# A first batch's near scores as one 64x64 product per head, and a new written-out order of the first 34 steps

## The chip, the core and the metric

The kernel runs on one core of a Trainium2 chip. The metric is the device time of one execution in microseconds. The core has a matrix engine (TensorE, PE in the profile; PEld is its loading of stationary operands), a vector engine (VectorE, DVE), an activation engine (ScalarE, ACT), a general engine (GpSimd, POOL), and a queue engine (SyncE, SP) whose instructions here only start DMA transfers. Each engine executes its own list of instructions strictly in the order in which it was written; semaphores make it wait for other engines. What stands behind a waiting instruction waits too.

## The reference

The computation is attention of two kinds over q, k, v of 8 batches, 8 heads, 576 positions, 64 elements a head, added up, followed by a two-layer network on all 4608 tokens.

```python
def _attn_ref(q, k, v):
    ...
    q_d = q.reshape(B, H, Sd, factor, D).mean(axis=3)      # and k_d, v_d; factor is 4
    out_d = sm_attn(q_d, k_d, v_d)                          # softmax attention on 144 means
    out_up = np.repeat(out_d, factor, axis=2)
    mask = np.abs(pos[:, None] - pos[None, :]) < factor     # near: 7 keys a query
    scores = scale * np.matmul(q, k.transpose(0, 1, 3, 2))
    scores = np.where(mask, scores, -1000000000.0)
    ... # softmax
    out_local = np.matmul(attn, v)
    return (out_up + out_local).astype(np.float32)

def _moe_ref(x, w_in, w_out, alpha):                        # x: 4608 x 512
    h = x @ w_in                                            # 512 x 2048
    g = np.maximum(h, 0.0) + alpha * np.minimum(h, 0.0)
    return (g @ w_out).astype(np.float32)
```

The two weight matrices arrive as 8-byte floats.

## The kernel before

**Steps of the network.** The tokens are cut into 18 chunks of 256, and the 2048 hidden columns into 8 pairs of 128-wide blocks, which gives 144 steps s = 0 to 143: chunk s // 8, pair s % 8. A step is `hidden` (24 matmuls of 128x256 into one of two PSUM banks, L971), `below` (ACT, L977) and `leak` (DVE, L993), which together apply the sloped activation, `split` (ACT, L999) and `spill` (POOL, L1005), which cut the result into a high and a low part, and `product` (12 matmuls of 128x512, L1033). High and low parts take the place of full float32 products: three matmuls for each. Since there are two banks for `hidden`, the `hidden` of step s + 2 can begin only when the `leak` of step s has read its bank.

**Weights.** Each pair's block of w_in (named `i0` to `i7`) and w_out (`o0` to `o7`) is loaded as raw 8-byte words (two DMAs, tile `raw`, three slots in turn) and turned into high and low parts by four operations: `convert` (ACT, L316), `bits` (DVE, L326), `upper` (ACT, L330) and `lower` (DVE, L336). `convert` writes a scratch tile, `temp`, of which there is one; the next `convert` waits until `bits` has read it. A slot of `raw` is free for the next load when `bits` has read it.

**First batch.** Tokens of batch 0 go first, since step 0 needs them. Their attention is done in four pairs of heads, `p0` to `p3`, with operations named `p0.turn00` and so on: `load0` and `load1` (q and k, tile `fqk`), `load2` (v, tile `fv`), `load3` (v in windows of 70 rows, tile `vw`), `turn` (PE transposes, tile `f0T` for q and `f1T` for k) and `turned` (ACT copies them to `qb` and `kT`), `near` (the masked near scores on PE, 9 windows of 64 queries and 70 keys, in two groups of 7 and 2, tile `fs`), `shift`, `near_exps` and `weights` (softmax, DVE and ACT), `over` and `kept` (turning the weights, tiles `fpt` and `fpT`), `near_weigh` (product with v, tile `fpv`), and beside them the 144-wide attention (`fold`, `flip`, `operands`, `scores`, `peak`, `exps`, `invert`, `scaled`, `across`, `held`, `weigh`, `store`). `join`, `high` and `low` put both together into `xx`, the operand of `hidden`. In `near` (L546 to L556), both heads of a pair lie on the 128 partitions, 64 each. The queries are put into `qb` block-diagonally: a window is 128 columns, of which the first 64 hold head 0 on partitions 0 to 63 and zeros below, the last 64 zeros and head 1 on partitions 64 to 127. One product of 128 by 128 with the 70 keys gives both heads' scores.

**Later batches** use other code: the near part on DVE (units `u3`, `u4`, ..., operations `multiply`, `total`, `first`, `weigh`, `gather`, `last`, lines L805 to L869) and the 144-wide part in pieces named `d10` (batch 1, pair 0), `d11` and so on, with their own loads (tile `ld`).

**Order.** Every operation has a due time in steps. The functions are called in the order of these times, which fixes the order on every engine and on SP's queue. For the first 34 steps (`HORIZON`) the due times come from the table `ORDER`, a list of 1027 names; behind it they come from rules, which the change does not touch.

Of the kernel before, what the change touches and what calls it, by code (L numbers as in the profile page):

```python
# [55 lines left out]
d10.load.0 o0.upper p0.invert p0.fold_v p1.near0 p0.scaled d10.load.1 o0.lower p0.kept0 p0.kept1 d10.load.3 p1.load3
p0.across0 p1.shift0 i1.convert p0.across1 p0.over2 o1.load p1.shift1 p0.held1 p0.near_weigh0 p0.kept2 i1.bits
p1.near_exps0 p3.load0 p1.near_exps1 p0.held0 p2.turn00 p1.weights i1.upper p0.weigh p2.turned00 p3.load1 d10.fold.0
p1.flip p0.store d10.fold.1 p2.turn10 p1.operands p0.near_weigh1 p2.turned10 o2.load i1.lower p2.turn04 d10.load.4
p2.turn14 d10.load.2 p2.turned04 p2.fold0 p1.scores p2.load2 p2.turned14 p2.fold1 p3.load2 p2.near0 o1.convert  # L60
p1.peak p1.fold_v p1.exps i2.load o1.bits p1.invert p0.join0 i3.load o1.upper p3.turn00 p2.shift0 p1.scaled
p0.near_weigh2 o1.lower p2.flip p2.near_exps0 p1.across1 p0.high0 p0.join2 p2.operands p0.low0 p1.across0 p1.held1
p0.join1 d10.fold.4 p2.near1 p1.held0 p0.high1 p0.low1 p1.over0 p3.turned00 p2.shift1 d10.fold.2 p2.near_exps1
p1.over1 p1.kept0 p2.weights d10.fold.3 p1.over2 p1.kept1 p3.turn04 p1.kept2 p3.turn10 p3.fold0 p3.turned04
# [1168 lines left out]
```

## Time and profile before

| | us |
|---|---|
| runs | 940.55, 941.21, 2989.08 |
| median | 941.21 |
| profiled execution: its time | 941.03 |
| profiled execution: span from first to last instruction | 939.2 |
| PE busy | 905.7 (96%) |
| DVE busy | 775.4 (83%) |
| POOL busy | 539.5 (57%) |
| ACT busy | 425.1 (45%) |
| chain that ended last, by engine | PE 73%, DVE 15%, ACT 4% |

The execution lasted 1.8 us longer than the span that its profile covers. The span has two parts: the first 86 us, in which batch 0's attention is made and the first weights are decoded, and the steps behind, in which PE hardly rests. A group of instructions shows its busy time, then the mean duration of one in ns, then the idle time ahead of it and who ended that. A row of the timeline that ends in square brackets tells how long the engine stood idle ahead of the instruction, and for whom.

### The profile page before, as it was taken

What the parts mean: (1) busy time and instruction counts of PE and PEld (TensorE: products, weight loads), DVE (VectorE), ACT (ScalarE), POOL (GpSimd) and SP (SyncE); (2) the same over time, 40 slices, a digit from 0 to 9 for tenths busy, and PEclk for the clock granted to TensorE, in tenths of its full rate; (3) what the DMA queues carried; (4) which work ended last, traced back from release to release, by engine and by line L of the source; (5) the groups of instructions that cost most, each with busy time, mean ns of one, the idle gap of its engine ahead of it and who ended that gap; (6) DMA issues with size and microseconds to landing.
All of it is one profiled execution on the core that took longest, in us unless ns stands there. A gap on an engine that the chain in (4) does not pass through costs nothing.

```text
span 939.2 us, 17607 instructions
## 1 busy us (share of the span) xinstructions
PE 905.7 (96%) x6402; PEld 833.4 (89%) x6402; DVE 775.4 (83%) x1389; ACT 425.1 (45%) x1069; POOL 539.5 (57%) x683
## 2 busy tenths in 40 slices
PE   5788999999999999999999999999999999999998
PEld 5676889898998999999999999999999999999997
DVE  5667679999997799998999889899998899997111
ACT  5588764524453453444443434444444442323221
POOL 2033476748757658667667476677657654525221
PEclk9998999999999999999999999999999999999999
DMA  7976733433343322522432433332424322210000
GB/s 176 209 237 199 261 95 87 132 111 100 105 129 101 90 83 69 157 83 83 129 98 73 133 91 105 105 105 71 139 85 117 107 72 66 78 35 24 1 24 22
DMA packets 63194, 98.25 MB, mean 105 GB/s; under 512 B 23556, under 2 KB 28932, under 8 KB 63108
## 3 DMA queue, kind: packets, MB, share of 16 engines
q1 hardware_dynamic: 62916, 96.88, 34.8%
q8 instruction: 50, 0.82, 0.4%
q10 hardware_dynamic: 192, 0.26, 0.1%
q14 instruction: 36, 0.29, 0.1%
HBM read 87.67 MB, written 9.44 MB: 103 GB/s over the span
## 4 chain that ended last, share of the span: by engine, by line
PE 73%; DVE 15%; ACT 4%; SPq 2%; DMA 2%; POOL 2%; issue 1%; ACTq 0%; DVEq 0%; POOLq 0%
PE h L971 33%; PE o L1033 32%; DVE qk L805 3%; DVE ls L809 3%; DVE t L993 2%; PE s L390 2%; DVE lb L866 2%; DVE pv L863 2%; PE pv L424 2%; ACT temp L316 1%; PE xp L875 1%; PE pT L414 1%; DMA raw<-in_moe_w_in 1%; DMA raw<-in_moe_w_out 1%; DVE xf L887 1%
## 5 line engine op out<-in xcount | busy, mean ns | idle before, releaser
L971 PE MATMUL h<-xx,wih 128*128 128x256 f32 x2304 | 332.7, 278 | 3.8 <-DVE t L993 3.0
L1005 POOL TENSOR_TENSOR gl<-t,gh 128x512 fp32r<-128x512 f32 x142 | 182.5, 1285 | 263.8 <-ACT gh L999 248.4
L971 PEld LDWEIGHTS h<-xx,wih 128*128 128x128 f32 x2304 | 297.9, 192 | 10.8 <-ACT woh L330 2.5
L993 DVE SCALAR_TENSOR_TENSOR t<-t,rise,h 128x256 f32<-128x256 f32 x288 | 124.8, 475 | 86.2 <-ACT t L977 85.7
L1033 PE MATMUL o<-woh,gh 128*128 128x512 f32 x576 | 184.0, 390 | 0.4 <-ACT sg L1040 0.4
L1033 PE MATMUL o<-woh,gl 128*128 128x512 f32 x576 | 177.6, 379 | 1.1 <-POOL gl L1005 1.1
L1033 PE MATMUL o<-wol,gh 128*128 128x512 f32 x576 | 177.5, 379 | 0.0
L971 PE MATMUL h<-xx,wil 128*128 128x256 f32 x1152 | 176.1, 276 | 0.0
L999 ACT CAST gh<-t 128x512 fp32r<-128x512 f32 x144 | 89.4, 621 | 181.1 <-PE o L1033 88.1
L977 ACT ACTIVATE t<-h 128x512 f32<-128x512 f32 x144 | 85.9, 596 | 160.4 <-PE h L971 130.1
L368 POOL TENSOR_TENSOR ld<-ld 72x256 f32<-72x256 f32 x167 | 124.4, 745 | 48.9 <-DMA ld<-in_q 29.6
L971 PEld LDWEIGHTS h<-xx,wil 128*128 128x128 f32 x1152 | 152.2, 192 | 0.0
L809 DVE TENSOR_REDUCE ls<-qk 128x12 f32<-128x768 f32 (+1 forms) x126 | 135.7, 1082 | 2.4
L1033 PEld LDWEIGHTS o<-woh,gl 128*128 128x128 f32 x576 | 108.8, 189 | 16.9 <-POOL gl L1005 1.5
L1033 PEld LDWEIGHTS o<-wol,gh 128*128 128x128 f32 x576 | 108.9, 189 | 14.9
L1033 PEld LDWEIGHTS o<-woh,gh 128*128 128x128 f32 x576 | 99.8, 190 | 11.2 <-issue 2.2
L866 DVE TENSOR_TENSOR lb<-lb,pv 128x384 f32<-128x384 f32 x168 | 94.8, 564 | 4.6
L805 DVE TENSOR_TENSOR qk<-k,qp 128x768 f32<-128x768 f32 (+1 forms) x78 | 83.5, 1076 | 0.3 <-ACT qp L799 0.2
L863 DVE TENSOR_TENSOR pv<-v,lb 128x1152 f32<-128x1152 f32 x84 | 79.5, 952 | 2.4
L189 POOL TENSOR_TENSOR xx<-xf,xx 128x256 fp32r<-128x256 f32 (+3 forms) x47 | 43.7, 934 | 25.2 <-ACT xx L901 25.2
L805 DVE TENSOR_TENSOR qk<-k,lb 128x768 f32<-128x768 f32 (+1 forms) x48 | 51.6, 1078 | 0.0
L887 DVE TENSOR_TENSOR xf<-xp,od 128x128 f32<-128x128 f32 (+3 forms) x110 | 39.9, 414 | 5.5 <-POOL xx L189 3.0
(148 smaller groups left out, 1009.8 us busy)
## 6 DMA issues: line engine op xcount, KB each, us to landing
...
raw<-in_moe_w_in SPq DMA_DIRECT2D x16, 512.0 KB
raw<-in_moe_w_out SPq DMA_DIRECT2D x16, 512.0 KB
ld<-in_q SPq DMA_DIRECT2D x56, 144.0 KB
ld<-in_k SPq DMA_DIRECT2D x56, 144.0 KB
ld<-in_v SPq DMA_DIRECT2D x56, 144.0 KB
```

The costliest lines, as they stand in the source:

```text
L368: e.tensor_tensor(lv[:, :, 0:128], lv[:, :, 0:128], lv[:, :, 128:256], op=ALU.add)
L805: nc.vector.tensor_tensor(st["qk", half, d0][:, :nd], window(tiles[u, "k"], half, d0, nd), st["qp", half].unsqueeze(1).to_broadcast([128, ...
L809: nc.vector.tensor_reduce(out=st["s"][:, half, d0:d0 + nd, :].rearrange("p a b -> p (a b)"), in_=st.pop(("qk", half, d0))[:, :nd].rearrang ...
L863: nc.vector.tensor_tensor(st["pv", half, d0][:, :nd], window4(tiles[u, "v"], half, d0, nd), prob(half, d0, nd), op=ALU.mult)
L866: nc.vector.tensor_tensor(st["acc"], st["acc"], st["pv", half, d0][:, i], op=ALU.add)
L887: nc.vector.tensor_tensor(xf.rearrange("p a t (s e) -> p e t a s", e=2)[:, par, k0:k0 + nk], tp.rearrange("p (t s e a) -> p e t a s", t=4, ...
L971: nc.tensor.matmul(ph[:, j], w[:, m, 128 * o:128 * o + 128], x[:, part, m], start=(i == 0), stop=(i == 11))
L977: nc.scalar.activation(t, hs[st], AF.Relu, scale=-1.0)
L993: nc.vector.scalar_tensor_tensor(t[:, j], t[:, j], rise[:, f:f + 1], h[:, j], op0=ALU.mult, op1=ALU.add)
L999: nc.scalar.copy(gh, t)
L1005: (nc.vector if f"s{st}.split" in ON_VECTOR else nc.gpsimd).tensor_tensor(gl, t, f32(gh), op=ALU.subtract)
L1033: nc.tensor.matmul(outs[c][m], g[:, j, 128 * m:128 * m + 128], wo[w][n][:, :, o].rearrange("p e a -> p a e"), start=(f == 0 and i == 0), s ...
```

## The change

The near scores of the first batch are written as two products of 64 by 64 a window, one for each head, in place of one of 128 by 128. `qb` loses its zero blocks (half its size, no memsets on DVE), and each `turned` of q is one ACT operation on 128 partitions in place of two on 64. The table `ORDER` has the same 1027 names in another order. In the diff, the table is cut to its first line.

```diff
 ORDER = """
-clear p0.load0 masks p0.load1 i0.load p1.load0 p0.turn00 p0.load3 p0.turn04 p0.turned00 p0.fold0 p0.turned04
...
+p0.load0 masks p0.load1 clear p0.load2 p1.load0 p1.load1 p0.turn00 p0.turn04 p0.turned00 i0.load p0.fold0
...
 """.split()
...
-        qb = st.tile([128, NWIN, 2, WIN], F32, name="qb")
-        nc.vector.memset(qb[0:64, :, 1, :], 0.0)
-        nc.vector.memset(qb[64:128, :, 0, :], 0.0)
+        qb = st.tile([128, NWIN, WIN], F32, name="qb")
...
             def turned(x, t0):
                 ps = s.pop(("turn", x, t0))
                 if x == 0:
-                    for e, r in enumerate(halves):
-                        nc.scalar.mul(
-                            qb[r, :, e, :].rearrange("p w (a t) -> p w a t", t=8)[:, :, :, t0:t0 + 4],
-                            ps[r].rearrange("p (t w a) -> p w a t", t=4, w=NWIN), SCALE)
+                    nc.scalar.mul(qb.rearrange("p w (a t) -> p w a t", t=8)[:, :, :, t0:t0 + 4],
+                                  ps.rearrange("p (t w a) -> p w a t", t=4, w=NWIN), SCALE)
...
                 for j in range(nw):
                     w = w0 + j
-                    nc.tensor.matmul(ps[:, KEYS * j:KEYS * j + KEYS], qb[:, w].rearrange("p e i -> p (e i)"),
-                                     kT[:, WIN * w:WIN * w + KEYS], start=False, stop=(j == nw - 1))
+                    for r in halves:
+                        nc.tensor.matmul(ps[r, KEYS * j:KEYS * j + KEYS], qb[r, w], kT[r, WIN * w:WIN * w + KEYS],
+                                         start=False, stop=(j == nw - 1))
```

The order shifts on every engine. Three places follow. The first is SP's queue around the load of the weight block i1 (`raw0_1`; `raw1` is a block of w_out). `fqk2` is q and k of pair 2, `fqk3` those of pair 3, `fv` and `vw` are v, `ld1_0` loads for batch 1. Before:

```order
L496 DMA fqk1_159<-in_k 72x8x64 x2
L274 DMA raw1_0_210<-in_moe_w_out 128x2048 x2
L514 DMA vw2_214<-in_v 70x9x64 x2
L501 DMA fv0_230<-in_v 72x2x512
L501 DMA fv1_237<-in_v 72x2x512
L514 DMA vw3_249<-in_v 70x9x64 x2
L270 DMA raw0_1_261<-in_moe_w_in 128x2x1024 x2
L496 DMA fqk2_281<-in_q 72x8x64 x2
L496 DMA fqk2_281<-in_k 72x8x64 x2
L358 DMA ld1_0_0_324<-in_q 72x512
L358 DMA ld1_0_1_343<-in_q 72x512
L358 DMA ld1_0_3_350<-in_k 72x512
```

Now the same stretch of SP's queue reads:

```order
L512 DMA vw0_190<-in_v 70x9x64
L274 DMA raw1_0_218<-in_moe_w_out 128x2048 x2
L499 DMA fv1_221<-in_v 72x2x512
L512 DMA vw2_239<-in_v 70x9x64 x2
L358 DMA ld1_0_0_252<-in_q 72x512
L358 DMA ld1_0_1_269<-in_q 72x512
L358 DMA ld1_0_3_289<-in_k 72x512
L494 DMA fqk2_297<-in_q 72x8x64 x2
L494 DMA fqk2_297<-in_k 72x8x64 x2
L270 DMA raw0_1_353<-in_moe_w_in 128x2x1024 x2
L494 DMA fqk3_376<-in_q 72x8x64 x2
L358 DMA ld1_0_4_405<-in_v 72x512
```

The q and k of pair 2 now stand ahead of i1, and the q of pair 3 directly behind it, where before the loads of batch 1, one `vw` and the weight block o1 came first.

The second place is ACT's list around the `convert` of the weight block o1 (`raw1_1`). Before, the exponentials of pair 1 (`fdp1`) stood behind it, and the copies of pair 1's turned weights (`fpT1`) further behind than shown:

```order
L544 COPY kT_114<-f1T20_429 128x72x4
L540 ACTIVATE qb_111<-f0T24_452 64x9x8x4 x2
L544 COPY kT_114<-f1T24_459 128x72x4
L316 ACTIVATE temp_121<-raw1_1_372 128x1024
L609 ACTIVATE fdp1_500,fdsm1_494<-fsd1_471,fdnb1_493 96x144 x3
L611 ACTIVATE fdsm1_494<-fdsm1_494 96x3
L330 ACTIVATE woh0_81<-temp_121 128x2x2x256
L618 ACTIVATE fdp1_500<-fdp1_500,fdrs1_495 96x144 x3
L661 ACTIVATE fp2_524,fsm2_522<-fs20_483,fmx2_521 128x70 x7
L721 CAST xx0_550<-fxs00_510 128x2x128
```

Now, on ACT, from the `convert` of i1 (`raw0_1`) to that of o1 and two rows on:

```order
L316 ACTIVATE temp_152<-raw0_1_353 128x1024
L540 COPY kT_112<-f1T20_466 128x72x4
L537 ACTIVATE qb_111<-f0T24_476 128x72x4
L606 ACTIVATE fdp1_497,fdsm1_472<-fsd1_453,fdnb1_471 96x144 x3
L608 ACTIVATE fdsm1_472<-fdsm1_472 96x3
L540 COPY kT_112<-f1T24_503 128x72x4
L681 COPY fpT1_528<-fpt10_488 70x512
L330 ACTIVATE wih0_79<-temp_152 128x4x256
L681 COPY fpT1_528<-fpt14_519 70x512
L316 ACTIVATE temp_152<-raw1_1_407 128x1024
L615 ACTIVATE fdp1_497<-fdp1_497,fdrs1_473 96x144 x3
L681 COPY fpT1_528<-fpt18_539 70x128
```

The exponentials and two of the three copies of pair 1 now stand ahead of the `convert` of o1.

The third place is DVE's list in the first steps of the network: the `leak` of step n reads the bank `hn` and writes `tn`; `raw0_5` is i5, in two halves (`temp051` and `temp050`), `raw1_4` is o4. Before:

```order
L993 SCALAR_TENSOR_TENSOR t0_1021<-t0_1021,rise_78,h0_942 128x256 x2
L336 SCALAR_TENSOR_TENSOR wil2_1029<-temp_121,wih2_1028 128x4x256
L326 SCALAR_TENSOR_TENSOR temp051_1086<-raw0_5_896,temp_121 128x512
L993 SCALAR_TENSOR_TENSOR t1_1041<-t1_1041,rise_78,h1_988 128x256 x2
L336 SCALAR_TENSOR_TENSOR wil2_1029<-temp051_1086,wih2_1028 128x2x256
L326 SCALAR_TENSOR_TENSOR temp050_1107<-raw0_5_896,temp_121 128x512
L326 SCALAR_TENSOR_TENSOR temp_121<-raw1_4_835,temp_121 128x1024
L336 SCALAR_TENSOR_TENSOR wil2_1029<-temp050_1107,wih2_1028 128x2x256
L993 SCALAR_TENSOR_TENSOR t2_1145<-t2_1145,rise_78,h2_1055 128x256 x2
```

Now DVE has there:

```order
L990 SCALAR_TENSOR_TENSOR t0_1051<-t0_1051,rise_78,h0_965 128x256 x2
L326 SCALAR_TENSOR_TENSOR temp051_1068<-raw0_5_931,temp_152 128x512
L326 SCALAR_TENSOR_TENSOR temp050_1103<-raw0_5_931,temp_152 128x512
L990 SCALAR_TENSOR_TENSOR t1_1109<-t1_1109,rise_78,h1_1022 128x256 x2
L336 SCALAR_TENSOR_TENSOR wil2_1013<-temp050_1103,wih2_1012 128x2x256
L336 SCALAR_TENSOR_TENSOR wil2_1013<-temp051_1068,wih2_1012 128x2x256
L326 SCALAR_TENSOR_TENSOR temp_152<-raw1_4_858,temp_152 128x1024
L990 SCALAR_TENSOR_TENSOR t2_1162<-t2_1162,rise_78,h2_1073 128x256 x2
```

Both halves of i5 now go through `bits` ahead of the `leak` of step 1; the `bits` of o4 still stands ahead of the `leak` of step 2.

More of the change, by code (lines that the diff above doesn't have):

```diff
@@ L56 @@
[L56 to L64, printed above, removed]
-p1.near_weigh1 p3.turned10 p3.turn14 i2.convert p1.near_weigh0 d10.load.5 p3.fold1 p2.scores p3.turned14 p3.near1
@@ L116 @@
-d20.turn.1 s.below.20 d21.flip d20.turned.1 s.hidden.21 d22.fold.0 s.leak.20 d21.operands u5.scaled.1 d22.load.2
-u5.total.0.5.2 s.send.1.1 u5.shift u5.exps s.hidden.22 u5.weights d22.fold.1 u5.load_q.6 u5.first.0 d22.fold.2
-u5.weigh.0.1.3 u4.flip.0 u5.weigh.0.4.1 u5.gather.0.1.0 u5.gather.0.1.1 s.product.17 u4.join.0 d22.load.3
-u5.gather.0.1.2 u4.place.0.0 d22.load.4 u5.gather.0.4.0 d22.load.5 u4.place.0.1 u5.multiply.1.0.3 d20.weigh
-s.split.19 d21.scores d20.store s.spill.19 u5.multiply.1.3.2 u4.flip.1 s.product.18 d21.peak u5.far.0 s.below.21
@@ new lines @@
+u3.place.0.0 u3.place.0.1 u4.first.0 u3.flip.1 d21.load.2 d20.flip u4.weigh.0.1.3 s.product.14 d20.operands
+d21.fold.0 u3.join.1 u4.far.0 u4.weigh.0.4.1 d21.load.3 u3.place.1.0 u4.gather.0.1.0 d20.scores u4.gather.0.1.1
+u4.gather.0.1.2 s.hidden.15 d20.peak u3.place.1.1 u4.gather.0.4.0 d20.exps u4.far.1 u4.weigh.1.1.3 s.hidden.16
+u4.weigh.1.4.1 s.below.15 d20.invert u4.last.0 d20.scale s.leak.15 d21.fold.2 u4.first.1 s.split.15 d21.fold.3
+u4.gather.1.1.0 u4.load_kv.5.v d20.turn.0 s.below.16 u4.gather.1.1.1 s.spill.15 d20.turn.1 d20.turned.0 s.leak.16
@@ new lines @@
+u5.weights u4.place.0.0 d22.load.2 s.leak.19 u4.place.0.1 d22.load.3 u5.first.0 d21.scores u5.weigh.0.1.3
+s.hidden.21 u5.weigh.0.4.1 u5.gather.0.1.0 d22.fold.2 d21.peak u5.gather.0.1.1 d21.exps u5.gather.0.1.2 u4.flip.1
+s.product.16 d22.load.4 u5.far.0 u4.join.1 u5.multiply.1.0.3 u4.place.1.0 d22.load.5 s.send.1.1 d21.invert
+u5.gather.0.4.0 d21.scale u5.total.1.0.3 d22.fold.3 s.product.17 s.split.18 u4.place.1.1 d23.load.0 u5.last.0
+u5.multiply.1.3.2 s.spill.18 u5.multiply.1.5.2 d21.turn.0 s.split.19 d22.fold.4 d21.turn.1 s.below.20 s.product.18
@@ new lines @@
+u5.total.1.3.2 u6.scaled.0 s.spill.19 u5.load_kv.6.k d21.turned.0 u5.total.1.5.2 d21.turned.1 s.leak.20 d22.fold.5
+s.below.21 d22.flip u5.shift~1 s.split.20 u5.flip.0 s.leak.21 d23.fold.0 d22.operands s.hidden.22 u5.join.0
+u5.exps~1 s.spill.20 u5.weights~1 u5.place.0.0 u5.weigh.1.1.3 u5.far.1 d21.weigh s.below.22 s.product.19 d21.store
+u5.first.1 s.leak.22 d23.load.1 u5.place.0.1 u5.gather.1.1.0 u5.weigh.1.4.1 u5.gather.1.1.1 d22.scores s.split.21
+u5.gather.1.1.2 s.spill.21 s.product.20 d22.peak u5.gather.1.4.0 d22.exps u5.last.1 u6.multiply.0.0.3 u6.scaled.1
@@ L155 @@
+s.split.31 d32.fold.2 s.spill.31 d32.load.5 s.hidden.34 s.below.33 s.leak.33 s.hidden.35 s.product.30 s.split.32
+s.product.31 s.spill.32 s.below.34 s.leak.34 s.stage.3.0 s.stage.3.1 s.send.3.0 s.split.33 s.product.32 s.spill.33
+s.below.35 s.leak.35 s.split.34 s.product.33 s.send.3.1 s.spill.34
 """.split()
```

173 lines of the change are left out of this document (85 added, 88 removed).

## The prediction

> **What bounds the kernel now.** I read the busy time by stretches first: 20 us each at the start, and one long one. Columns: stretch, its length, then PE, PEld, DVE, ACT, POOL busy with counts, the granted TensorE clock, the DMA share, GB/s.
>
> ```profile
> 0.00:20.00 20.00, 10.89 (x58) 9.82 (x58) 10.86 (x26) 10.08 (x20) 6.58 (x27) 1.00 0.75 178
> 20.00:40.00 20.00, 13.99 (x96) 12.16 (x97) 13.04 (x25) 12.43 (x31) 1.38 (x2) 1.00 1.05 203
> 40.00:60.00 20.00, 16.14 (x105) 13.68 (x104) 13.65 (x26) 15.64 (x50) 5.21 (x7) 1.00 0.90 274
> 60.00:80.00 20.00, 17.35 (x121) 14.12 (x119) 15.81 (x31) 17.21 (x47) 2.25 (x3) 1.00 0.49 163
> 300.00:939.00 639.00, 634.69 (x4482) 589.36 (x4480) 529.21 (x948) 253.63 (x629) 376.91 (x454) 1.00 0.28 83
> ```
>
> From 300 us on PE rests 4.3 us of 639, so only the start and PE's few gaps can give time. In the start no engine is full: PE rests 9.1, 6.0, 3.9 and 2.7 us in the four stretches, while the DMA share is near 1 from 20 to 60. Next, the chain of waits up to step 0 (start, length, what) and the waits of PE behind it (total, times, longest):
>
> ```profile
> 23.21 9.93 DMA raw<-in_moe_w_in
> 36.08 8.34 DMA raw<-in_moe_w_out
> 61.32 0.86 PE fs L555 x4
> 64.04 2.89 PE fs L555 x14
> 82.10 1.36 ACT temp L316
> 86.39 6.90 PE h L971 x48
> PE h L971 <- DVE t L993: 3.0, 2, 2.1
> PE o L1033 <- POOL gl L1005: 1.1, 1, 1.1
> ```
>
> Loads of weights carry the chain to 44 us, then ACT and PE alternate until the first `hidden` at 86.4. The near scores of pair 3 are on it with 3.75 us. Behind 86.4 PE waits about 5 us in all, 2.1 of them in one place:
>
> ```profile
> 99.06 0.38 PE L1033 MATMUL o<-woh,gh 128*128 128x512 f32 x1
> ...
> 101.43 0.38 PE L1033 MATMUL o<-woh,gl 128*128 128x512 f32 x1
> 103.90 0.68 PE L971 MATMUL h<-xx,wih 128*128 128x256 f32 x4 [2.09 <-DVE t L993]
> ```
>
> So the time is the start of step 0, plus PE's work, plus PE's gaps behind it.
>
> **The instructions that change.** First PE's prices, from the timeline:
>
> ```profile
> 56.67 1.12 PE L696 MATMUL fpv<-fpT,vw 70*64 70x64 f32 x16
> 62.11 1.23 PE L635 MATMUL fdv<-fth,fvd 72*64 72x144 f32 x8
> 63.84 3.09 PE L555 MATMUL fs<-kT,qb 128*128 128x70 f32 x14
> 81.28 1.15 PE L696 MATMUL fpv<-fpT,vw 70*64 70x64 f32 x32
> ```
>
> A float32 product is two passes here (14 records for 7 windows), 3.09 / 14 = 221 ns a pass, 18 passes for a pair of heads: 4.0 us. Now there are 36 passes with 64 columns and 70 keys. No row shows products on one half of the rows; the nearest are `fpv`, 70 rows, 64 columns, the two heads on different output partitions: 1.12 / 16 = 70 ns. The other end is `fdv`, 144 long: 1.23 / 8 = 154 ns. I take 70, since the size is that of `fpv` nearly: 36 x 0.070 = 2.5 us, 1.5 less a pair. Bounds: 36 ns a pass (the last row, 1.15 / 32), 2.7 less; 154 ns, 1.5 more.
>
> A rule speaks against it. Both heads write one bank from different halves of the rows. The Trainium skill, "TensorEngine Tiling (Array Packing)", says under "Gotcha 1: PSUM Pressure": "Different row tiles cannot access same PSUM bank simultaneously". By that sentence the two would go one after the other; no row shows it, and it is the first rival.
>
> For ACT and the rest:
>
> ```profile
> L540 ACT ACTIVATE qb<-f0T 64x288 f32<-64x288 f32 x16 | 6.5, 404 | 6.8 <-PE f0T L533 6.7
> L544 ACT COPY kT<-f1T 128x288 f32<-128x288 f32 x8 | 3.7, 457 | 0.5 <-PE f1T L533 0.4
> ```
>
> Sixteen copies of 404 ns become eight on 128 partitions, at 457 like those of k: 6.5 - 3.7 = 2.8 us of ACT, 0.7 a pair. The two memsets on DVE lie ahead of the first q and k, where nobody waits for DVE, and are worth nothing.
>
> **The start of step 0.** What moved is whose load and whose turn comes first. The issue sizes and ACT's and PE's waits for loads:
>
> ```profile
> raw<-in_moe_w_in SPq DMA_DIRECT2D x16, 512.0 KB
> fqk<-in_q SPq DMA_DIRECT2D x8, 144.0 KB
> fv<-in_v SPq DMA_DIRECT2D x4, 288.0 KB
> vw<-in_v SPq DMA_DIRECT2D x7, 157.5 KB
> ld<-in_q SPq DMA_DIRECT2D x6, 144.0 KB
> 21.85 1.35 ACT L316 ACTIVATE temp<-raw 128x1024 f16<-128x1024 bf16 x1 [1.10 <-DMA raw<-in_moe_w_out]
> 33.22 1.35 ACT L316 ACTIVATE temp<-raw 128x1024 f16<-128x1024 bf16 x1 [5.53 <-DMA raw<-in_moe_w_in]
> 35.08 0.71 PE L533 MATMUL f0T<-ident,fqk 72*128 72x72 f32 x4 [4.78 <-DMA fqk<-in_q]
> 44.52 1.35 ACT L316 ACTIVATE temp<-raw 128x1024 f16<-128x1024 bf16 x1 [3.01 <-DMA raw<-in_moe_w_out]
> 46.08 0.71 PE L533 MATMUL f0T<-ident,fqk 72*128 72x72 f32 x4 [0.66 <-DMA fqk<-in_q]
> ```
>
> Between o0 (21.85) and i1 (33.22) stood two `vw`, two `fv` and i1 itself: 2 x 315 + 2 x 288 + 1024 = 2230 KB in 11.4 us, 196 KB a us. In SP's old order 6033 KB reach up to pair 2's q, now 5126: it should land 4.6 us sooner, where PE had stood 4.78. Pair 3's q: 8380 before, 6726 now, 8.4 us sooner. Against it, i1 has 6438 KB for 5745, 3.5 us later; o1 7894 for 8092, 1 sooner; pair 3's k 8956 for 8668, 1.5 later. The `vw` of pair 1, moved back most, has 8361 KB and should land near 46; it was first used at 56.67.
>
> So i1's hold on ACT gets later, but more work is done ahead of it and of o1's. What now stands ahead of the `convert` of o1 on ACT, where before it stood behind, and what went behind step 0's operands:
>
> ```profile
> L609 ACT ACTIVATE fdp<-fsd,fdnb 96x144 f32<-96x144 f32 x12 | 4.3, 375 | 0.0
> L684 ACT COPY fpT<-fpt 70x512 f32<-70x512 f32 x8 | 4.3, 584 | 0.3 <-PE fpt L678 0.2
> L678 PE MATMUL fpt<-ident,fp 128*70 128x128 f32 x36 | 9.1, 404 | 2.6 <-ACT fpT L684 1.3 <-DVE fxs L710 1.0 <-DVE fp L672 0.3
> ```
>
> Three exponentials (1.1), two copies (1.2) and 0.7 for `qb` of pair 3 leave the stretch behind o1; so does the `convert` of i4 (1.36, at 82.10 in the chain), now behind the `kd` copy, for which PE waits ahead of step 0. ACT has 4.4 us less there. PE has pair 1's turning of weights less (9.1 / 4 = 2.3), the small near group of pair 2 (0.9, as pair 3's in the chain) and 1.5 for pair 3: 4.7 less. Both engines carried that stretch, so step 0 can begin up to 4.5 us sooner, and 1 more if o1 lands sooner. Waits between the two will not all shrink: I take 4. Bounds: 6, and 0 if another load takes i1's place as the hold.
>
> **Behind step 0.** The 2.1 us wait: `hidden` of step 4 needs the bank that `leak` of step 2 reads, and that stood on DVE behind the `bits` of o4, whose `convert` waited on ACT for the scratch tile that i5's second `bits` still read. Now both halves of i5 are converted directly behind step 0's `below`, so the `bits` of o4 should end some 4 us sooner relative to step 0: the wait goes (2.1). PE is next held by nothing that I can see until step 8. From there on the order is another one, with PE's remaining waits (0.9 and 1.1 in the rows of waits, and smaller ones) made anew: I book +2 for holds of the size seen. Bounds -2, if none come back, and +5.
>
> The granted clock costs something too:
>
> ```profile
> 85.00:90.00 5.00, 5.00 (x30) 4.55 (x29) 3.93 (x8) 3.42 (x12) 2.86 (x5) 0.59 0.61 208
> ```
>
> Step 0's first matmuls run partly at half clock. `fpv` at 36 ns against 70 earlier says that PE was slow before 75 us as well, though the column reads 1.00. Step 0 lies in this stretch from 86.4 on; 0.41 of the clock is missing over 3.6 us, 1.5 us. I keep that cost as it is, and 1.5 either way as its bound.
>
> **The sum.** Against the profiled execution: 941.03 - 4 (start) - 2.1 + 2 = 936.9. Its time is 0.2 us under the median, so the forecast is 937. End to end the bounds are 941 - 6 - 2.1 - 2 - 1.5 = 929.4 and 941 - 0 + 5 + 1.5 = 947.5.
>
> **The rivals.**
>
> 1. The two heads' products run one after the other, since both write one bank from different rows. For it: no row shows two such products beside each other. Against: `fpv` overlaps its two heads in one bank. At 154 ns a pass, a pair takes 5.5 us in place of 2.5; pair 3's 3.0 us lie on the path: 940. The sentence of the Trainium skill's tiling page quoted above is this rival's rule.
>
> 2. The gain at the start is lost at the weights. Steps 4 to 7 need i4 to i7 as they come, while the DMA share behind step 0's start is near 1:
>
> ```profile
> 90.00:105.00 15.00, 12.91 (x106) 12.27 (x105) 10.64 (x16) 10.28 (x16) 7.29 (x10) 1.00 0.97 328
> ```
>
> If PE starts 4 us sooner but the blocks land no sooner, PE waits 4 us there: 941. Against: from 60 to 80 the share is 0.49, since loads waited for slots that DVE's `bits` free, and these get sooner with the rest.
>
> 3. Slower: DVE becomes the hold between steps 14 and 17. The order now puts the second half of unit `u4` (products, sums and the join of `u3`) between the `leak` of step 14 and that of step 15. DVE's busy time before it, and prices:
>
> ```profile
> 100.00:135.00 35.00, 32.90 (x242) 29.95 (x241) 24.71 (x39) 27.38 (x57) 18.87 (x23) 1.00 0.50 170
> L805 DVE TENSOR_TENSOR qk<-k,qp 128x768 f32<-128x768 f32 x12 | 11.2, 944 | 0.0
> L866 DVE TENSOR_TENSOR lb<-lb,pv 128x384 f32<-128x384 f32 x40 | 22.6, 564 | 1.0
> ```
>
> Added up from such rows this is about 17 us of DVE work between two `leak`s; before, the longest such stretch is about 10.5. PE has four `product`s and two `hidden`s (2.75 us, 99.06 to 101.81, and 3.45, half of 6.90) before it needs the bank: 17.9 and some transposes. It holds if DVE reaches step 14's `leak` less than about 3 us behind PE. If DVE comes 9 us late there, PE waits 6, and if units 5 to 7 take 1 each: 937 + 9 = 946. For it: the start moves PE ahead, not DVE. Against: DVE rests 10.3 us between 100 and 135, which the new order fills with `u3`, begun a step and a half sooner.
>
> **Chances.** Forecast 0.62, its own range 931 to 940; rival 1 0.13; rival 2 0.15; rival 3 0.10. The range 931 to 943 takes in the first two rivals and leaves out most of the third and the forecast's far end. Two per cent, about what a measurement of this kernel can tell from no change, is 18.8 us: 922.4 or 960.0. All of PE's rest in the first 80 us is 21.7, and the first loads need some of it; faster by 2% gets 0.02. Slower by 2% would take rival 3 in every unit, at twice its price: 0.02.
>
> **What the profile will show.** Right: a pass of the near scores at about 70 ns; the wait of PE for pair 2's q gone or near 1 us; the first `hidden` near 82.4; no wait of 2 us ahead of step 4; PE's waits behind it 4 us in all. Wrong: passes near 150 ns (rival 1); PE waiting for loads or decoded weights between 85 and 115 us (rival 2); `hidden` waiting for `leak` for several us between 160 and 200 (rival 3); or a first `hidden` at 86 or later, where ACT waits for i1 longer than it did, and the start was mis-sized.

## The result, and the profile after

The changed kernel takes 932.08 us (median of four runs, 930.93 to 932.68), beside 941.16 for the kernel before on the same chip (four runs, one of them a slow one of 2989.08 us that stays out of the ratio): a ratio of 0.9904, 95% interval 0.9885 to 0.9924. That is 9.1 us less. The forecast was 937, with a range of 931 to 943; the time lies in the range and on the side foretold, but the gain is more than twice the 4.2 us forecast, and it was made where the forecast was furthest off (below). The profiled execution took 930.93, 1.2 under the median, with a span of 929.2.

First the stretches of the changed kernel (columns as in the prediction: stretch, length, PE, PEld, DVE, ACT, POOL busy, granted clock, DMA share, GB/s):

```profile
0.00:20.00 20.00, 12.13 (x95) 10.41 (x96) 11.29 (x29) 9.07 (x19) 6.60 (x27) 1.00 0.85 208
20.00:40.00 20.00, 16.39 (x153) 12.73 (x153) 17.15 (x32) 14.95 (x40) 3.74 (x5) 0.66 0.97 223
40.00:60.00 20.00, 18.01 (x155) 13.96 (x149) 16.78 (x31) 17.33 (x60) 3.88 (x5) 0.58 0.98 277
60.00:80.00 20.00, 16.95 (x146) 14.17 (x145) 14.19 (x26) 17.41 (x44) 6.80 (x11) 0.65 0.66 211
```

From 0 to 40 us the queue moves 208 and 223 GB/s for 178 and 203 before. From 20 to 40 it does so with a DMA share of 0.97 where before had 1.05: the transfers that stand there now carry more for the same time.

The timeline of the changed kernel at the places that the prediction named: pair 2's q, the converts of i1 and o1, pair 3's near scores, and the start of step 0 (start, length, engine, line, operation; in brackets the idle time ahead):

```profile
28.06 0.74 PE L531 MATMUL f0T<-ident,fqk 72*128 72x72 f32 x4 [1.76 <-DMA fqk<-in_q]
33.81 1.35 ACT L316 ACTIVATE temp<-raw 128x1024 f16<-128x1024 bf16 x1 [3.30 <-DMA raw<-in_moe_w_in]
39.18 1.37 ACT L316 ACTIVATE temp<-raw 128x1024 f16<-128x1024 bf16 x1
51.20 1.90 PE L552 MATMUL fs<-kT,qb 64*64 64x70 f32 x28
74.96 1.22 PE L968 MATMUL h<-xx,wih 128*128 128x256 f32 x4
```

They stood at 35.08, 33.22, 44.52, 63.84 and, for step 0, at

```profile
86.32 1.22 PE L971 MATMUL h<-xx,wih 128*128 128x256 f32 x4
```

in the kernel before. Step 0 begins 11.4 us sooner, where 4 were forecast. From its start to the end of the span it takes 929.2 - 74.96 = 854.2 us, before 939.2 - 86.32 = 852.9: behind the start 1.3 us are given back. The waits of PE there, from the same view as in the prediction:

```profile
PE o L1030 <- POOL gl L1002: 3.4, 1, 3.4
PE o L1030 <- ACT sg L1037: 0.8, 2, 0.5
PE h L968 <- DVE t L990: 0.7, 2, 0.4
```

The waits for `leak` (3.0 us before, 2.1 of them ahead of step 4) are down to 0.7. In their place stands one wait of 3.4 us for a `spill` (tile `gl`), and behind it PE runs at half speed. The timeline of PE around it:

```profile
267.75 0.59 PE L1030 MATMUL o<-wol,gh 128*128 128x512 f32 x2
271.73 1.17 PE L1030 MATMUL o<-woh,gl 128*128 128x512 f32 x2 [3.39 <-POOL gl L1002]
272.69 1.06 PE L1030 MATMUL o<-woh,gh 128*128 128x512 f32 x2
273.55 1.06 PE L1030 MATMUL o<-wol,gh 128*128 128x512 f32 x2
274.40 1.01 PE L1030 MATMUL o<-woh,gl 128*128 128x512 f32 x2
275.25 0.61 PE L968 MATMUL h<-xx,wih 128*128 128x256 f32 x4
```

Two matmuls take 0.59 us ahead of the wait and 1.01 to 1.17 behind it. This is the `product` of step 29. Its last eight matmuls take 3.5 us (271.73 to 275.25); at full speed two start every 0.43 us, so the half speed costs 1.8 us.

### The profile page after: what moved, and what is told of

Its sections match the earlier page's. It is cut to its first block, busy times and chain, and to the rows that moved or that the text cites. A ratio compares the mean times of both kernels' runs of the same rounds, so it can differ in the third digit from the quotient of the medians.

```text
span 929.2 us, 17762 instructions
## 1 busy us (share of the span) xinstructions
PE 902.7 (97%) x6474; PEld 827.5 (89%) x6474; DVE 775.2 (83%) x1387; ACT 420.5 (45%) x1061; POOL 541.3 (58%) x683
## 4 chain that ended last, share of the span: by engine, by line
PE 71%; DVE 17%; DMA 3%; POOL 2%; SPq 2%; ACT 2%; issue 2%; ACTq 0%; DVEq 0%; POOLq 0%
PE h L968 32%; PE o L1030 32%; DVE ls L806 3%; DVE qk L802 3%; DVE t L990 2%; DVE pv L860 2%; DVE lb L863 2%; DMA raw<-in_moe_w_in 2%; PE s L390 2%; PE pv L424 1%; PE xp L872 1%; PE pT L414 1%; SPq L494 1%; DVE xf L884 1%; DMA fv<-in_v 1%
## 5 line engine op out<-in xcount | busy, mean ns | idle before, releaser
L189 POOL TENSOR_TENSOR xx<-xf,xx 128x256 fp32r<-128x256 f32 (+3 forms) x47 | 43.8, 936 | 10.5 <-ACT xx L898 10.4
L400 ACT ACTIVATE dp<-s,dnb 96x144 f32<-96x144 f32 x84 | 30.6, 370 | 33.3 <-DVE dnb L394 33.2
```

The costliest lines, as they stand in the source:

```text
L189: nc.gpsimd.tensor_tensor(o, a, b, op=ALU.subtract)
```

## The experiments

Each kernel is compared with the kernel before on its own chip; where times of different chips are set side by side, it is by these ratios. The table has, from each profile, the start of o1's `convert` on ACT, the start of step 0, the stretch between the two, and what is left of the span behind the start of step 0.

| kernel | o1's convert | step 0 | stretch | behind | median us | ratio to before |
|---|---|---|---|---|---|---|
| before | 44.52 | 86.32 | 41.8 | 852.9 | 941.2 | 1 |
| changed | 39.18 | 74.96 | 35.8 | 854.2 | 932.08 | 0.9904 (0.9885 to 0.9924) |
| e1: new products, old order | 41.99 | 82.26 | 40.3 | 853.1 | 940.68 | 0.9986 (0.9966 to 1.0005) |
| e2: new order, old products | 41.84 | 77.74 | 35.9 | 854.0 | 932.42 | 0.9889 (0.9869 to 0.9909) |
| e3: changed, loads in old sequence | 48.51 | 83.95 | 35.4 | 854.2 | 940.87 | 0.9993 (0.9974 to 1.0012) |
| e4: before, loads in new sequence | 42.11 | 84.78 | 42.7 | 853.6 | 941.58 | 1.0006 (0.9986 to 1.0025) |
| e6: new order to step 0, old behind | 43.09 | 77.57 | 34.5 | 854.0 | 933.28 | 0.9909 (0.9892 to 0.9926) |
| e7: old order to step 0, new behind | 41.81 | 83.39 | 41.6 | 854.1 | 941.63 | 0.9999 (0.9981 to 1.0017) |
| e8: changed, one load of windows sooner | 42.42 | 76.38 | 34.0 | 854.0 | 932.57 | 0.9900 (0.9884 to 0.9916) |
| e10: e3, pair 2's q and k first | 46.70 | 82.41 | 35.7 | 853.9 | 940.19 | 0.9983 (0.9972 to 0.9994) |
| e14: e10, next batch's q first | 46.88 | 81.97 | 35.1 | 854.4 | 939.18 | 0.9970 (0.9953 to 0.9987) |
| e16: e14, pair 3's q first | 44.55 | 81.35 | 36.8 | 854.1 | 939.72 | 0.9982 (0.9966 to 0.9999) |
| e11: changed, ACT's copies twice | 42.08 | 80.14 | 38.1 | 855.3 | 934.46 | 0.9923 (0.9906 to 0.9940) |
| e13: changed, i4's convert ahead | 41.20 | 76.76 | 35.6 | 854.8 | 933.36 | 0.9903 (0.9878 to 0.9928) |
| e5: changed, spill of step 29 sooner | 39.80 | 75.31 | 35.5 | 853.6 | 930.63 | 0.9877 (0.9862 to 0.9893) |
| e9: e5 and six more steps sooner | 39.66 | 75.48 | 35.8 | 851.3 | 928.70 | 0.9861 (0.9846 to 0.9875) |
| e15: e9, product 30 ahead of hidden 35 | 39.77 | 76.63 | 36.9 | 848.9 | 926.38 | 0.9839 (0.9816 to 0.9862) |

A profile is one of several executions. Those of e1 and e7 took 3.5 and 2.3 us less than their medians, so their step 0 usually begins nearer 86 than 82 or 83; those of e10 and e16 took 2.1 and 2.4 us less, and that of e11 took 2.8 us more. One more run, e12, leaves products out, was run once and is read for its rows alone. In all kernels but e9 and e15 the part behind the start is 853 to 855 us: the time is the start plus a constant.

**Which part of the change.** Theories: A, the sequence of the loads sets the start; B, the new products and copies; C, the order of the work on ACT and PE.

e1, the changed kernel with the old table:

```diff
 ORDER = """
-p0.load0 masks p0.load1 clear p0.load2 p1.load0 p1.load1 p0.turn00 ...     (the new table)
+clear p0.load0 masks p0.load1 i0.load p1.load0 p0.turn00 p0.load3 ...      (the old table)
```

> The 64x64 products and the one copy for qb, with the order of before in all steps. Theory A (the start is set by when loads land, so by the order of the loads): PE still waits about 4 us for pair 2's q near 35 us, and the first hidden starts 1.5 to 2.5 us sooner than 86.3, by the shorter passes of pair 3 (14 passes of 221 ns become 28 of 65) and the copies; 938 to 940 us. Theory B (the products and copies are what lets step 0 begin): first hidden at 80 or sooner, 931 to 934. Theory C (the order of the work on ACT and PE): as A, 84 to 85 and 938 to 940.

e2, the kernel before with the new table:

```diff
 ORDER = """
-clear p0.load0 masks p0.load1 i0.load p1.load0 p0.turn00 p0.load3 ...      (the old table)
+p0.load0 masks p0.load1 clear p0.load2 p1.load0 p1.load1 p0.turn00 ...     (the new table)
```

> The new order in all steps, with the block-diagonal 128x128 products, two copies and two memsets of before. Theories A and C: the first hidden near 77 to 79, since only 2 to 4 us of PE's work come back (four pairs at 1.6, part of it beside waits); 933 to 936 us. Theory B: first hidden at 83 or later, 938 or more.

e1 is 0.14% faster than before, with an interval that holds 1; e2 has all of the changed kernel's gain. Theory B falls. The pair of rows says why: of the stretch between o1's `convert` and step 0, first in the changed kernel, then with the old products, then one of the old near groups:

```profile
39.18:74.96 35.78, 30.74 (x277) 23.92 (x277) 27.45 (x49) 32.24 (x93) 9.08 (x14) 0.60 0.84 249
```
```profile
41.84:77.74 35.90, 33.62 (x245) 28.31 (x243) 27.22 (x49) 33.34 (x95) 9.55 (x14) 1.00 0.84 251
54.25 3.10 PE L555 MATMUL fs<-kT,qb 128*128 128x70 f32 x14
```

The new products and copies take 2.9 us off PE and 1.1 off ACT there, and the stretch keeps its length (35.8 and 35.9): PE rests 5.0 us of it where it rested 2.3.

e3 and e4 set the loads alone:

```diff
 (e3: the new table; the 37 loads ahead of s.hidden.0 change places with one another, and p0.fold_v goes behind p0.invert; only names of loads are shown)
-p0.load0 p0.load1 p0.load2 p1.load0 p1.load1 i0.load p0.load3 o0.load p1.load2 p2.load3 d10.load.0 d10.load.1 d10.load.3 p2.load0 p2.load1 i1.load p3.load0 d10.load.4 o1.load ...
+p0.load0 p0.load1 i0.load p1.load0 p0.load3 p1.load1 o0.load p2.load3 p0.load2 p1.load2 p3.load3 i1.load p2.load0 p2.load1 d10.load.0 d10.load.1 d10.load.3 p1.load3 o1.load ...
 (e4: the old table, with + for - and - for +; no other name moves)
```

> The changed kernel, with the loads ahead of step 0 in the sequence they had before (each takes the place of another load in the new order; the fold of pair 0's v goes back behind invert, since its load now comes later). Everything else as in the changed kernel. Theory A: PE waits for pair 2's q again, the converts of i1 and o1 wait for their loads as they did in before, and the first hidden is at 81 to 86; 937 to 942 us. Theory C (ACT and PE's order makes the gain): first hidden at 75 to 78, 932 to 934.

> The kernel before, with only the loads ahead of step 0 in the sequence of the new order (each takes the place of another load). Products, copies and every other step as before. Theory A: pair 2's q and o1 land 5 us or more sooner, the first hidden is at 77 to 81, 932 to 936 us. Theory C: loads land sooner but ACT and PE go through the same work in the same order behind them; first hidden at 83 to 86, 938 to 941. By the sum of the prediction (fixed 196 KB a us) the loads alone would give about 1 to 2 us.

With the old sequence of loads the new order loses everything (0.9993), and the new sequence gives the old order nothing (1.0006). Neither A nor C holds alone. The table splits the two: the stretch behind o1's `convert` is 34 to 37 us in every kernel with the new order, whatever the loads (38 where ACT's copies are doubled), and 40 to 43 in every kernel with the old. The loads move the other term, the start of o1's `convert`: in the new order it comes at 39 to 43 with the new sequence and at 48.5 with the old. In the old order it hardly follows: e4 has it at 42.11 (41.8 to 44.5 with the old sequence), with no wait for its load, since ACT came to it no sooner.

**The start or the steps behind it.**

```diff
 (e6: the new table up to s.hidden.0, then the names left over as the old table has them; e7: the other way round)
```

> The changed kernel, with the new order up to the hidden of step 0 and the order of before behind it. Theory A (the whole gain is the earlier start, and behind it the old order is as good as the new): first hidden at 75 to 77, then 853 us as in before: 928 to 932. Rival (what follows must fit the start: loads, bits and converts that the old order has later become PE's waits in steps 1 to 8): 935 to 940, with PE's waits behind step 0 at 9 us or more.

> The changed kernel, with the order of before up to the hidden of step 0 and the new order behind it. Theory A (the gain is the start): first hidden at 82 to 86, then 854 us as in the changed kernel: 938 to 942. Rival (a good part of the gain is in steps 1 to 33, as the prediction's 2.1 us wait ahead of step 4): 934 to 937.

e6 has the changed kernel's gain (0.9909; 933.28 us is 1.3 above theory A's range and far from the rival's), e7 none of it (0.9999). Behind the start, e6 has PE's old waits for `leak` again:

```profile
PE h L968 <- DVE t L990: 4.0, 4, 1.7
```

e7 has the 3.4 us wait for `gl` instead. The two rests are worth the same.

**Which loads the new order needs.** In e3 the engines stood for loads that the new order uses early: PE for pair 2's q, and DVE for the next batch's q (`ld`), whose `fold` now stands ahead of the `join` of pair 0:

```profile
34.47 0.71 PE L531 MATMUL f0T<-ident,fqk 72*128 72x72 f32 x4 [5.36 <-DMA fqk<-in_q]
37.92 0.55 DVE L368 TENSOR_TENSOR ld<-ld 72x256 f32<-72x256 f32 x1 [9.02 <-DMA ld<-in_q]
```

Four runs moved loads one after the other:

```diff
 (e8: the new table; only names of loads are shown)
-... d10.load.3 p2.load0 p2.load1 i1.load p3.load0 d10.load.4 o1.load d10.load.2 p3.load3 ...
+... d10.load.3 p3.load3 p2.load0 p2.load1 i1.load p3.load0 d10.load.4 o1.load d10.load.2 ...
 (e10, e14, e16: e3's sequence, each with one group more moved ahead)
-... p1.load2 p3.load3 i1.load p2.load0 p2.load1 d10.load.0 d10.load.1 d10.load.3 p1.load3 o1.load p3.load0 ...
+... p1.load2 p2.load0 p2.load1 p3.load3 i1.load d10.load.0 d10.load.1 d10.load.3 p1.load3 o1.load p3.load0 ...
+... p1.load2 p2.load0 p2.load1 d10.load.0 d10.load.1 p3.load3 i1.load d10.load.3 p1.load3 o1.load p3.load0 ...
+... p1.load2 p2.load0 p2.load1 d10.load.0 d10.load.1 p3.load3 i1.load d10.load.3 p3.load0 p1.load3 o1.load ...
```

> The changed kernel with one load moved: pair 3's windows of v (315 KB in pieces of 256 bytes) ahead of pair 2's q and k and the i1 block, about where before had them. By the prediction's fixed rate of 196 KB a us everything behind lands 1.6 us later, by the rate of such pieces in the trace of before (288 KB of q in 1.86 us, 155 KB a us) 2.0. If each us of landing is a us of the start: first hidden at 76.5 to 77.5, 933.5 to 934.5 us. If one such load sets the whole difference between the old and the new sequence: 937 or more. If there is slack: 932.

> The changed kernel with the old sequence of loads, as in the run that lost the whole gain (first hidden at 83.95, 940.9 us), except that pair 2's q and k go ahead of pair 3's windows and the i1 block. Theory A (the new order of work needs pair 2's q and k ahead of i1; the rest of the sequence matters little): pair 2's first transposes near 29 for 34.5, the convert of i1 near 36 for 40.7, o1 near 43 for 48.5, first hidden at 77 to 79; 933 to 936 us. Rival (o1's windows of pair 1, or the later k of pair 3 and i2, hold as much): 938 or more.

> As the run with pair 2's q and k first in the old sequence of loads (first hidden 82.41, 940.2 us), and with the first two loads of the next batch's q (288 KB) also ahead of pair 3's windows and i1. Theory A (in the new order DVE folds that q early; the fold stood 7.35 us for its load, behind it the join of pair 0, behind that ACT's cast and the convert of i1): the wait is gone or under 1.5 us, i1's convert at 34 to 37 for 38.9, o1's at 40 to 43 for 46.7, first hidden at 75.5 to 78.5, 932 to 935 us. Rival (the windows of pair 1 ahead of o1, or the late q and k of pair 3, hold the same work): first hidden at 80 or later, 937 or more.

> As the run before it (old sequence of loads, with pair 2's q and k and the next batch's q ahead of pair 3's windows and i1; first hidden 81.97, 939.2 us), with pair 3's q also ahead of pair 1's windows and the o1 block. Theory A (three loads that the new order uses early are the whole of the dependence): PE's 4.84 us wait for pair 3's q is under 2, o1's convert at 41 to 44 for 46.9, first hidden at 76 to 79, 932.5 to 936 us. Rival (a further load, pair 3's k or i2, comes next): first hidden at 79.5 or later, 936.5 or more.

e8 costs nothing that can be measured (0.9900 for 0.9904): a pair's windows ahead of pair 2's q do not make the difference. In the other three theory A missed, and the time lies where the rival had it. Each time the wait that was named went, and the next load that the new order uses early took its place. The longest waits of DVE, ACT and PE for loads in e10 (DVE for the next batch's q, and ACT behind it ahead of i1's `convert`), in e14 (pair 3's q) and in e16 (the i2 block):

```profile
35.96 0.56 DVE L368 TENSOR_TENSOR ld<-ld 72x256 f32<-72x256 f32 x1 [7.35 <-DMA ld<-in_q]
38.56 0.43 ACT L718 CAST xx<-fxs 128x256 fp32r<-128x256 f32 x1 [7.87 <-DVE fxs L707]
```
```profile
44.80 0.71 PE L531 MATMUL f0T<-ident,fqk 72*128 72x72 f32 x4 [4.84 <-DMA fqk<-in_q]
```
```profile
57.29 1.36 ACT L316 ACTIVATE temp<-raw 128x1024 f16<-128x1024 bf16 x1 [3.69 <-DMA raw<-in_moe_w_in]
```

In the changed kernel i2's `convert` starts at 48.35, without a wait. So no single load carries the gain; the sequence as a whole follows the order in which the engines now ask for data. Which smallest set would do stays open: with pair 2's q and k, the next batch's q and pair 3's q put first, step 0 still begins 6 us later than in the changed kernel (81.35 for 74.96).

**What shortens the stretch.** The stretch in the kernel before:

```profile
44.52:86.32 41.80, 33.61 (x257) 26.91 (x257) 28.24 (x52) 36.47 (x104) 11.23 (x16) 0.95 0.67 215
```

ACT is busy 36.5 of 41.8 us there and 32.2 of 35.8 in the changed kernel: 4.2 us less work and 1.8 less idle. e11 gave ACT work back, e13 took one operation of the prediction's list back onto ACT's way to step 0.

```diff
 (e11, in kept)
-                nc.scalar.copy(s["pT"][...], s.pop(("over", i))[:KEYS, 0:128 * nw])
+                ps = s.pop(("over", i))
+                for _ in range(2):
+                    nc.scalar.copy(s["pT"][...], ps[:KEYS, 0:128 * nw])
 (e13, the table)
-p3.near_weigh1 d11.fold.0 d10.operands i5.load i4.convert p3.near_weigh0
+p3.near_weigh1 d11.fold.0 i4.convert d10.operands i5.load p3.near_weigh0
```

> The changed kernel with ACT's copy of the turned weights (fpT, 13 of them) made twice, so that the same values are written again: by the rows of the changed kernel 3.7 us of ACT more between o1's convert and step 0, and 2.4 ahead of o1. Theory A (behind o1's convert ACT carries the start, so its work there counts one to one): the stretch from o1's convert to the first hidden grows from 35.8 to 39 or 39.5, the first hidden comes 3.5 to 6 later; 935.5 to 938 us. Rival (PE and ACT take turns, and ACT's idle takes it up): stretch under 37, 932 to 934. The run with the old products, 2.9 us of PE more in the same stretch, left its length as it was (35.9).

> The changed kernel with one move on ACT: i4's convert (1.36 us) back ahead of the qd and kd copies of the next batch, for which PE waits ahead of step 0, as it stood in before. Theory A (the convert was on the path to step 0 one to one): the stretch from o1's convert to the first hidden grows by 1.4, from 34 to 36 in the runs so far to 35.5 to 37.3, PE waits for kd ahead of step 0; 933 to 933.8 us. Rival (PE has other work there): no change, 932.

```profile
42.08:80.14 38.06, 31.65 (x263) 24.38 (x259) 26.93 (x49) 34.96 (x100) 9.22 (x14) 0.50 0.77 240
```

In e11 ACT is busy 2.7 us more in the stretch and the stretch is 2.3 longer, short of theory A's 39 and over the rival's 37. But this profile is of the slowest of four runs, 2.8 us over their median, so the 2.3 may be the spread of single runs. The ratios (0.9923 beside 0.9904) point the same way, and their intervals overlap. Whether ACT's work there counts is not shown. e13 changes nothing that can be measured (stretch 35.6, ratio 0.9903), but its interval is 2.4 us either way, so 1.36 us could hide in it. PE waits 0.50 us for `kd` there, and nothing in this profile gives the convert of i4 its 1.36 us:

```profile
74.66 1.75 PE L390 MATMUL s<-kd,qd 128*96 128x144 f32 x6 [0.50 <-ACT kd L385]
```

**The near products by themselves.**

```diff
 (e12)
-                    for r in halves:
+                    for r in halves[:1 + (j == nw - 1)]:
                         nc.tensor.matmul(ps[r, KEYS * j:KEYS * j + KEYS], qb[r, w], kT[r, WIN * w:WIN * w + KEYS],
```

> The changed kernel without the second head's near products, but for the last window of each group (the near weights of the odd heads of the first batch are then wrong): 16 passes a group of seven windows for 28. If the two heads overlap in the array, the 16 passes take nearly as long as the 28 (1.5 to 1.9 us), over 100 ns a pass. If they go one after the other (the first rival of the prediction), 16 passes take 16/28 of 1.9 us, 1.1 us, 65 to 70 ns a pass.

```profile
53.49 1.89 PE L552 MATMUL fs<-kT,qb 64*64 64x70 f32 x16
```

16 passes take 1.89 us, as long as the 28 of both heads (1.90): the second head's passes cost nothing beside the first's. The speed was the same, for the product with the mask just ahead (128x490, L547) takes 0.78 us in both. The two heads run in the array at once, into one bank.

**What is given back at 270 us.**

```diff
 (e5, the new table)
-d31.flip s.split.29 u7.gather.0.4.0 ... s.product.28 d32.load.2 d30.store u7.far.1 ... d31.exps s.spill.29 u7.gather.1.4.0 ...
+d31.flip s.split.29 s.spill.29 u7.gather.0.4.0 ... s.product.28 d32.load.2 d30.store u7.far.1 ... d31.exps u7.gather.1.4.0 ...
 (e9, from there)
-... d30.store u7.far.1 u7.last.0 u7.weigh.1.4.1 u7.first.1 d31.scores u7.gather.1.1.0 s.split.30 u7.gather.1.1.1 d32.fold.1 d31.peak u7.gather.1.1.2 d31.exps u7.gather.1.4.0 u8.multiply.0.0.3 s.spill.30 s.below.31 s.product.29 s.leak.31 s.below.32 u7.last.1 s.leak.32 ...
+... d30.store s.split.30 s.spill.30 s.below.31 u7.far.1 u7.last.0 u7.weigh.1.4.1 s.leak.31 u7.first.1 d31.scores u7.gather.1.1.0 s.below.32 u7.gather.1.1.1 s.leak.32 d32.fold.1 d31.peak u7.gather.1.1.2 d31.exps u7.gather.1.4.0 u8.multiply.0.0.3 s.product.29 u7.last.1 ...
 (e15, from there)
-... s.below.33 s.leak.33 s.hidden.35 s.product.30 s.split.32 ...
+... s.below.33 s.leak.33 s.product.30 s.hidden.35 s.split.32 ...
```

> The changed kernel with one step moved: the spill of step 29 (the subtraction that makes gl, on POOL) directly behind the split of step 29, where the new order puts it behind 14 more POOL operations of the last unit and of pair d31. Theory A (the 3.39 us wait of PE at 271.7, and the half clock behind it, 8 products and passes at 1.06 us for 0.59, are what the order gives back): the wait goes, PE's gaps behind step 0 shrink to 1 us, 926.5 to 928.5 us. Rival (PE is held there by more than the one subtraction, for example by the leak or by POOL's later work that now comes 1.3 us later): the wait stays in part or moves, 930 to 932.

> The changed kernel with nine places of its order changed near 270 us: the spill of step 29 directly behind its split; split and spill of step 30 and the below of step 31 behind the store of pair d30; the leak of step 31 ahead of unit 7's first.1; below and leak of step 32 ahead of pair d31's peak. What the run with the spill alone left: PE waited 2.92 us for the leak of step 31, whose below stood on ACT behind d31's exponentials and, through them, behind DVE's sums of unit 7. Theory A (the gap and its half clock cost PE 3.4 plus about 1.7 us, and only the order of these steps makes them): no wait over 1 us behind step 0; 926.5 to 928.5 us, ratio to before 0.984 to 0.986. Rival (PE has too little other work there; the wait moves to a later step): 930 to 931.

> The kernel with the steps near 270 us put sooner (928.7 us), and there the product of step 30 ahead of the hidden of step 35, so that PE has 2.6 us of other work while the leak of step 33 is late. Theory A: the 1.67 us wait at 278 goes; 926.8 to 927.5 us. Rival (PE stands later for the split of step 31): 928 to 929.

In e5 the wait for `gl` goes, and PE stands 2.92 us for the `leak` of step 31 instead; the rival was right. In e9 that one goes too, and 1.67 us are left at `hidden` of step 35, so that its theory A, no wait over 1 us and 928.5 us at most, is narrowly missed. First e5, then e9:

```profile
273.29 0.68 PE L968 MATMUL h<-xx,wih 128*128 128x256 f32 x4 [2.92 <-DVE t L990]
273.81 0.61 PE L968 MATMUL h<-xx,wil 128*128 128x256 f32 x4
274.26 1.64 PE L968 MATMUL h<-xx,wih 128*128 128x256 f32 x8
275.69 1.06 PE L968 MATMUL h<-xx,wil 128*128 128x256 f32 x4
```
```profile
278.15 0.68 PE L968 MATMUL h<-xx,wih 128*128 128x256 f32 x4 [1.67 <-DVE t L990]
```

In e15 no wait over 0.5 us is left behind step 0:

```profile
PE o L1030 <- ACT sg L1037: 0.9, 2, 0.5
PE h L968 <- DVE t L990: 0.8, 2, 0.4
```

It takes 926.38 us (0.4 below theory A's range), ratio 0.9839 (0.9816 to 0.9862), which is faster than both the kernel before and the changed one (0.9885 to 0.9924). The part behind step 0 shrinks from 854.2 to 848.9: 5.3 us. PE's brackets behind step 0 add up to 5.7 us in the changed kernel and 2.7 in e15, so 3.0 are the waits themselves. Of the other 2.3, 1.8 are the half speed behind the 3.4 us wait, by the rows around 271.73; the rest was not taken apart.

## Why the prediction was right and wrong

**Near passes: right, and worth nothing.** 70 ns a pass were forecast; the row of pair 3 gives 1.90 / 28 = 68. The first rival falls: the two heads' passes overlap in one bank, which e12 shows directly. By the Trainium skill, "TensorEngine Tiling (Array Packing)", under "Gotcha 1: PSUM Pressure", they could not; here the measurement decides. The step's second half, that pair 3's shorter pass lies on the way to step 0, is not borne out: e2, without it, has the same stretch, and the chain of waits up to step 0 goes through pair 3's near scores neither in e2 nor in the changed kernel.

**ACT's copies: right in size** (the eight take 3.3 us for 6.5, 3.2 less for the 2.8 forecast), and not visible in the time: e2 has none of it.

**Start of step 0: the step that failed.** The prediction wrote "Both engines carried that stretch, so step 0 can begin up to 4.5 us sooner, and 1 more if o1 lands sooner", took 4 and bounded it at 6. The profiles show 11.4, which is two terms, and both were sized too small. That the time still lies in the range is luck: the start broke its bound, and the low end was made of other gains, in the holds and the clock, that did not come.

The stretch behind o1's `convert` fell by 6.0 us. ACT's work in it fell by 4.2, near the 4.4 listed, and then the prediction went on: "Waits between the two will not all shrink: I take 4." ACT's idle time shrank too, by 1.8. "Both engines carried that stretch" does not hold for PE: e2 has 2.9 us more of PE's work in it and the same length. That the new order shortens it is shown, through which of its moves is not. And the list agrees in its sum by luck more than in its parts. Rows of ACT in the stretch, before and changed:

```profile
L316 ACT ACTIVATE temp<-raw 128x1024 f16<-128x1024 bf16 x6 | 8.2, 1362 | 5.3 <-DMA raw<-in_moe_w_out 3.0 <-DVE temp L326 1.8 <-DMA raw<-in_moe_w_in 0.5
L609 ACT ACTIVATION_READ_ACCUMULATOR fdp<-fsd,fdnb 96x1 f32 x9 | 1.9, 208 | 0.0
```
```profile
L316 ACT ACTIVATE temp<-raw 128x1024 f16<-128x1024 bf16 x6 | 8.2, 1361 | 1.9 <-DVE frs L668 1.6 <-DMA raw<-in_moe_w_out 0.3
L606 ACT ACTIVATION_READ_ACCUMULATOR fdp<-fsd,fdnb 96x1 f32 x6 | 1.2, 205 | 0.0
```

Six converts stand in it in both, so i4's 1.36 us did not go; the accumulator reads that belong to the three exponentials, 0.7 us, I had not listed.

o1's `convert` itself came 5.3 us sooner, where I had 1. Part of the 5.3 is the spread of single runs: over the profiles with the new order and the new sequence (the changed kernel, e2, e5, e6, e9, e12, e13, e15) it starts at 40.8 on average, and e1 and e7, whose runs were 3.5 and 2.3 us under their medians, have 42 where the kernel before has 44.5. By the medians the start moved by 9.1 + 1.3 = 10.4 us, so 10.4 - 6.0, about 4, belong here. The working that failed is the fixed rate. I priced every load at 196 KB a us. By it pair 2's q was to come 4.6 us sooner and i1 3.5 later; the rows above have 7.0 sooner and 0.6 later. (One sum of mine was wrong besides: up to the windows of pair 1 the new sequence has 8668 KB, not 8361. They still came sooner than the 46 that I had: PE waited 0.86 us for them and went on at 43.85.) SP issued o1's load at

```profile
35.64 0.87 SPq L274 DMA_DIRECT2D raw<-in_moe_w_out  x2
```
```profile
30.43 1.32 SPq L274 DMA_DIRECT2D raw<-in_moe_w_out  x2
```
```profile
34.37 1.56 SPq L274 DMA_DIRECT2D raw<-in_moe_w_out  x2
```

before, in the changed kernel, and in e8. Over ten profiles with the new sequence ahead of it the issue is at 31.7 on average (30.4 to 33.6), over four with the old at 34.5 (33.5 to 35.6): 2.8 us for 198 KB less, where the fixed rate gives 1.0.

e8 points at the kind of load that is dear: one pair's windows, 315 KB in pieces of 64 floats, put ahead of it move it from 31.7 to 34.4, 2.7 us or about 117 KB a us, where the fixed rate gives 1.6. That is one profile against a mean with a spread of 1.5 either way, which does not tell 117 from 196. The single packets of the trace do: between 20 and 45 us of the kernel before, one of 256 bytes took 27 ns on average on its DMA engine and one of 2048 bytes 133 ns, which over 16 engines is 154 and 247 KB a us. The Trainium skill, "DMA: Bandwidth & Descriptors", under "Specifications", names 512 bytes as the least transfer for the full rate; the trace agrees, with 154 KB a us beside 247.

Ahead of o1 the new sequence has two pairs' windows less (630 KB), and pair 3's q (288 KB, written in pieces of 64 floats too) and one load of the next batch (144 KB) more. At 154 KB a us for such pieces and 247 for the last, that is an estimate of 342 / 154 - 144 / 247 = 1.6 of the 2.8 us. What is left of the 2.8, and the 1.2 of the 4 that lie behind the issue, was not taken apart: where ACT stood for o1's load (e5, e6, e9, e12, e13), 8.4 to 11.5 us passed from its issue to the `convert`. Nor is a us of o1's issue a us of the time: e8 issues it 2.7 us later and is as fast.

What I did not see at all is that the two terms need each other. I had the load sequence as a gain of its own, pair 2's q 4.6 us sooner and pair 3's q 8.4. e4 shows that it is worth nothing without the new order of work, and e3 that the new order is worth nothing without it.

**Ahead of step 4: right.** The 2.1 us wait is gone in the changed kernel and in e7, and is back, with 1.7, in e6.

**New holds: the waits came out, the speed behind one was not counted.** Behind the start the forecast had -2.1 + 2 = -0.1; it is +1.3. PE's brackets there add up to 5.9 us before and 5.7 in the changed kernel, so their balance is as booked (the 4 us in all that the prediction named as a sign of being right is not), but by luck: the old ones of 0.8 to 2.1 us went, and a single one of 3.4 us came, where holds of about 1 us had been the measure. What was put at nothing is the speed behind so long a wait: PE's busy time from step 0 on grew from 842.7 to 844.2 us, with 1.8 of half speed at step 29. The hold comes from where the new table puts one POOL subtraction, and behind that two `leak`s with their `below`s (e5, e9). The bound of +5 held it.

**Rivals 2 and 3** fell. Between step 0 and 181 us PE's timeline in the changed kernel has no wait above 0.3 us, so neither weights nor DVE's sums hold it, and from 160 to 200 there are two waits for `leak`, of 0.36 and 0.38 us. DVE was the hold behind the `leak` that e5 uncovered, but sixteen steps later than the third rival put it.

**The clock of step 0** is as before: the first four matmuls of `hidden` take 1.22 us in both.
